# Attention and two feed-forward blocks on one core: how the folded matrix W is multiplied, and where weight blocks lie in SBUF

## The chip, the core and the metric

One core of a Trainium2 chip. The metric is device time of one execution in microseconds; the kernel before takes 933.91 us in the median of three runs. TensorE (PE) multiplies, VectorE (DVE), ScalarE (ACT) and GpSimd (POOL) work on tiles in SBUF, SyncE (SP) issues all the loads and stores.

## The reference, cut to what matters

```python
def _attn_ref(q, k, v):                 # B, H, S, D = 4, 8, 576, 64, all float32
    scores = scale * np.matmul(q, k.transpose(0, 1, 3, 2))
    mask = (rel >= 0) & (rel < 128)
    scores = np.where(mask, scores + bias, -1e9)      # bias: slope per head times distance
    attn = softmax(scores)
    return np.matmul(attn, v)

def _moe_ref(x, w1, w2, w3, w_out):     # x: 2304 x 512, d_ff 1024
    h = ((x @ w1) * (x @ w2)) @ w3
    return h @ w_out

def _moe2_ref(x, w_in, w_out):          # d_ff 2048
    h = x @ w_in
    return (h * np.clip(h + 3.0, 0.0, 6.0) / 6.0) @ w_out
```

The output is `_moe2_ref(_moe_ref(attention))`. In the text w_in and w_out of the last block are v_in and v_out.

## The kernel before

**Numbers.** Products are taken in float32 precision by splitting an operand into a high part (fp32r) and a low part, the remainder: `mm3` (L46) multiplies high by high, high by low and low by high, three matmuls for one. `split` (L68) makes the parts: a cast on ScalarE, a subtraction on another engine. Weights come from the host as 64-bit floats; `unpack` (L51) makes float32 of them in place, one step on ScalarE (L60) and two on VectorE (L61, L62). A block of 128 x 1024 weights thus costs five operations: three to unpack, two to split.

**Attention.** 16 head pairs (n = 0 to 15, four per batch), each in six slots (`attn_slot`): scores s_n_j for five blocks of 128 queries, softmax (biased scores pr, their minimum mn, sums sm, reciprocals rc), POOL's scaling by the reciprocal (L228), transposes (pt, th), the product with v (X_n_h for the two heads), and the split into xh and xl. The first four pairs are `whole`: their products are float32 matmuls on unsplit operands, such as s at L189 and X at L273; the other pairs use split operands. For whole pairs q is loaded to partitions 0 to 63, and k to both halves (L131 to 134); the other half of q is zeroed.

**W.** w3 and w_out are folded once: W = w3 @ w_out, 1024 x 512. `wo_unit` (L357) unpacks and splits four blocks of w_out to woh and wol, `w3_unit` (L361) eight blocks of w3 to w3h and w3l, `w_half` (L381) multiplies: eight row blocks wps0 to wps7, each eight times `mm3` at 512 columns. The result is split to Wh and Wl. `w12_unit` (L369) unpacks and splits the eight blocks of w1|w2.

**Order.** The list `queue` (L412) says in which order the 20 raw blocks are loaded: four of w_out, five of w3, three of w1|w2, three of w3; the other five blocks of w1|w2 follow in a loop at L449. They pass through two raw buffers (`rawp`, bufs=2): a load waits until the block two places earlier has been split. `work` spreads unpacking and W over 26 slots of attention (L438). The framework's scheduler then orders all instructions of each engine by priorities of its own; every engine, and SP's queue, works strictly in that order.

**Stages.** For each batch b and each half of its tokens, `ab_unit` multiplies x with a block of w1|w2 (two accumulators of 24 matmuls in all, in the two banks of `ps_mm`; asb on ScalarE and VectorE, then the split g), and `y_unit` multiplies with W. Attention of the next batch is interleaved. At the last batch the first three blocks of v_in|v_out and the first tokens of y are loaded and split ahead (L540 to 548), through one buffer (`dec`). The second block of layers then runs `h_unit` (h, rl, g2) and `o_unit` two behind it, for five blocks of 512 tokens; during the first of them the other 13 blocks of v_in|v_out are loaded, through the two buffers of `dec2`, and split, the low parts by POOL and VectorE in turn (L604 to 609).

## Time and profile before

| what | us |
|---|---|
| median of 3 runs | 933.91 (933.59 to 934.82) |
| the profiled execution | 938.28 |
| its span, first to last instruction | 936.5 |
| TensorE busy in the span | 892.5 (95%) |
| VectorE, ScalarE, POOL busy | 453.9, 416.2, 169.2 |
| mean granted clock of TensorE, share of full | 0.974 |

The profile is of one execution, and its times are those of that execution; the runs shown were timed without it. A matmul's end is modelled, so the spacing of starts tells what one costs; "idle before" is what an engine stood still ahead of an instruction, and the releaser is what it waited for last. PEclk is the granted clock of TensorE; 1.00 is the upper of its two levels (2.4 GHz), 0.50 the lower (1.2 GHz).

### The profile page before, as it was taken

To read this page: it belongs to the slowest core of one execution; us is meant where nothing else is said; L and a number is where in the kernel's file an instruction comes from. 1 tells how busy PE (TensorE), PEld (TensorE's weight loads), DVE (VectorE), ACT (ScalarE), POOL (GpSimd) and SP (SyncE) were. 2 spreads that over 40 slices of the span, in tenths; PEclk is the share of its full clock that TensorE was granted. 3 is DMA by queue.
4 is the path that set the end of the run, shared out by engine and by line. 5 is a ranking of instruction groups with operands and counts; after the bars stand their busy time and mean duration, and the time that the engine had idled before them with its cause. 6 is when DMAs were issued, how large, how long until landed. Compare 5 with 4: busy or idle time off the path is not lost.

```text
span 936.5 us, 13589 instructions
## 1 busy us (share of the span) xinstructions
PE 892.5 (95%) x5280; PEld 802.7 (86%) x5280; DVE 453.9 (48%) x940; ACT 416.2 (44%) x868; POOL 169.2 (18%) x230
## 2 busy tenths in 40 slices
PE   4798888999999999999999989999999999999998
PEld 3686667999999999999999978888888888888897
DVE  5768787647474656643422187842223222222232
ACT  5746666646464556543432266642223222222232
POOL 3311433312332333321020222230002001000000
PEclk8898878999999999999999989999999999999999
DMA  9674753212323233000430265410002000100010
GB/s 242 217 243 146 232 154 108 54 47 54 90 64 90 64 83 71 20 21 13 149 103 13 100 205 192 158 67 23 1 1 69 0 1 1 45 1 0 1 45 24
DMA packets 23473, 75.20 MB, mean 80 GB/s; under 512 B 2928, under 2 KB 8560, under 8 KB 18800
## 3 DMA queue, kind: packets, MB, share of 16 engines
...
q14 instruction: 24, 0.20, 0.1%
...
## 4 chain that ended last, share of the span: by engine, by line
PE 80%; DVE 1%; DMA 1%; ACT 1%; issue 0%; POOL 0%; DVEq 0%; ACTq 0%
PE o L47 7%; PE o L49 7%; PE o L48 7%; PE h L47 7%; PE h L49 7%; PE h L48 7%; PE ab L47 7%; PE ab L48 7%; PE ab L49 7%; PE y L47 3%; PE y L49 3%; PE y L48 3%; PE X L273 3%; PE pt L246 2%; PE s L191 1%; PE s L192 1%
## 5 line engine op out<-in xcount | busy, mean ns | idle before, releaser
L47 PE MATMUL ab<-xh,w12h 128*128 128x288 f32 x512 | 156.5, 306 | 1.7 <-ACT xh L68 0.9
L48 PE MATMUL ab<-xl,w12h 128*128 128x288 f32 x512 | 153.0, 299 | 0.0
L49 PE MATMUL ab<-xh,w12l 128*128 128x288 f32 x512 | 152.6, 298 | 0.0
L577 DVE SCALAR_TENSOR_TENSOR rl<-rl,h 128x512 f32<-128x512 f32 (+1 forms) x80 | 50.5, 633 | 178.6 <-ACT rl L576 178.6
L576 ACT ACTIVATE rl<-h,three 128x512 f32<-128x512 f32 (+1 forms) x80 | 51.5, 645 | 185.7 <-PE h L49 183.9
L47 PE MATMUL h<-yh,v2h 128*128 128x512 f32 (+1 forms) x320 | 118.7, 371 | 4.0 <-ACT v2h L68 4.0
L49 PE MATMUL h<-yh,v2l 128*128 128x512 f32 (+1 forms) x320 | 118.2, 369 | 0.0
L48 PE MATMUL h<-yl,v2h 128*128 128x512 f32 (+1 forms) x320 | 118.2, 369 | 0.0
L47 PE MATMUL o<-v2h,g2h 128*128 128x512 f32 x288 | 113.8, 395 | 0.0
L48 PE MATMUL o<-v2l,g2h 128*128 128x512 f32 x288 | 113.2, 393 | 0.0
L49 PE MATMUL o<-v2h,g2l 128*128 128x512 f32 x288 | 109.6, 394 | 0.0
L47 PEld LDWEIGHTS ab<-xh,w12h 128*128 128x128 f32 x512 | 97.5, 191 | 3.1 <-DVE asb L471 1.1
L48 PEld LDWEIGHTS ab<-xl,w12h 128*128 128x128 f32 x512 | 97.9, 191 | 0.0
L49 PEld LDWEIGHTS ab<-xh,w12l 128*128 128x128 f32 x512 | 97.7, 191 | 0.0
L228 POOL TENSOR_SCALAR pr<-pr,rc 128x256 f32<-128x256 f32 (+1 forms) x128 | 68.5, 554 | 156.2 <-DVE rc L221 132.9
L69 DVE TENSOR_TENSOR g2l<-rl,g2h 128x512 fp32r<-128x512 f32 (+1 forms) x80 | 57.9, 723 | 42.9 <-ACT g2h L68 42.7
L47 PE MATMUL y<-g,Wh 128*128 128x288 f32 x256 | 75.4, 298 | 0.0
L48 PE MATMUL y<-g,Wh 128*128 128x288 f32 x256 | 75.1, 295 | 0.0
L49 PE MATMUL y<-g,Wl 128*128 128x288 f32 x256 | 74.9, 295 | 0.0
L47 PEld LDWEIGHTS h<-yh,v2h 128*128 128x128 f32 x320 | 60.2, 188 | 15.2 <-ACT v2h L68 4.4
L48 PEld LDWEIGHTS h<-yl,v2h 128*128 128x128 f32 x320 | 60.3, 188 | 11.2
L519 POOL TENSOR_TENSOR yl<-yraw,yh 128x1024 fp32r<-128x1024 f32 (+1 forms) x10 | 23.3, 2348 | 256.3 <-ACT yh L518 256.3
...
## 6 DMA issues: line engine op xcount, KB each, us to landing
raww<-in_w_dram SPq DMA_DIRECT2D x16, 1024.0 KB, 5.3
rawv<-in_w2x_dram SPq DMA_DIRECT2D x16, 1024.0 KB, 4.7
...
rawwo<-in_wo_dram SPq DMA_DIRECT2D x4, 1024.0 KB, 8.9
yraw<-yT SPq DMA_DIRECT2D x4, 1024.0 KB, 5.2
```

Source lines behind the costliest of these rows:

```text
L47: nc.tensor.matmul(ps, lh, rh, start=first, stop=False)
L48: nc.tensor.matmul(ps, lh, rl, start=False, stop=False)
L49: nc.tensor.matmul(ps, ll, rh, start=False, stop=last)
L69: lo_eng.tensor_tensor(out=lo, in0=src, in1=f32(hi), op=ALU.subtract)
L191: nc.tensor.matmul(o, sp1["qs"][:, qc], sp1["kh"][:, kc], start=True, stop=False)
L192: nc.tensor.matmul(o, sp1["qs"][:, qc], sp1["kl"][:, kc], start=False, stop=True)
L228: nc.gpsimd.tensor_scalar(out=o, in0=o, scalar1=rc[:, 2 * j + h : 2 * j + h + 1], scalar2=1.0, op0=ALU.mult, op1=ALU.mult)
L246: nc.tensor.transpose(ps[:, o : o + P], prob[n, j][:, h, c : c + P], ident)
L273: nc.tensor.matmul(X[:, c0 : c0 + nq], l, r, start=bank not in seen, stop=last[bank] == idx, skip_group_check=True)
L519: nc.gpsimd.tensor_tensor(out=yl[:, c, 0:n], in0=t[:, c, 0:n], in1=f32(yh[:, c, 0:n]), op=ALU.subtract)
L576: nc.scalar.activation(rl[:, 0:n], ps[:, 0:n], AF.Relu, bias=three[:, 0:1], scale=1.0)
L577: nc.vector.scalar_tensor_tensor(out=rl[:, 0:n], in0=rl[:, 0:n], scalar=6.0, in1=ps[:, 0:n], op0=ALU.min, op1=ALU.mult)
```

## The change

1. **W.** w3 and w_out are only unpacked (`unpack` gets an output tile), and `w_half` multiplies them as whole float32 operands: 64 matmuls of 512 columns in place of 192. woh, wol, w3h, w3l and their splits are gone.
2. **Places.** A pool `blk` has 16 places of 4 KB per partition, hi0 to hi7 and lo0 to lo7, which live to the end of the program. w_out lies in hi4 to hi7 and w3 in lo4 to lo7 (four blocks at a time) until W is made; then w1|w2 blocks 4 to 7 take these. Blocks 3 to 10 of v_in|v_out take the places of w1|w2 blocks 0 to 7 when those are done with.
3. **Raw buffers.** Three in the first stage (`rawx` adds one). Four blocks of w1|w2 come ahead of the last three of w3, and the work is spread over 20 slots in place of 26 (`WEND`).
4. **v_in|v_out.** Blocks 0 to 10 and the first tokens of y are made during the last batch, after the units listed in `AT`, through two buffers; the rest during the first h units. All low parts are made by VectorE.
5. **k of whole pairs** is loaded to one half of the partitions; the other half is zeroed once, by POOL.

```diff
-    def unpack(raw):
+    def unpack(raw, out=None):
...
+        out = w0 if out is None else out.bitcast(I32)
         nc.vector.scalar_tensor_tensor(
-            out=w0, in0=w1, scalar=3, in1=w0, op0=ALU.logical_shift_left, op1=ALU.bitwise_or
+            out=out, in0=w1, scalar=3, in1=w0, op0=ALU.logical_shift_left, op1=ALU.bitwise_or
         )
...
+    blk = ctx.enter_context(tc.tile_pool(name="blk", bufs=1))
...
+    rawx = raw_ctx2.enter_context(tc.tile_pool(name="rawx", bufs=1, side="right"))
...
-            for a in range(1 if whole(n) and nm == "q" else 2):
+            for a in range(1 if whole(n) else 2):
...
     def wo_unit(i):
-        c = slice(2 * i, 2 * i + 2)
-        split(flat(woh[:, c, :]), flat(wol[:, c, :]), unpack(rawt.pop(("wo", i))), nc.vector)
+        t = blk.tile([P, 2, DM], F32, tag=f"hi{KH + i}", name=f"wov{i}")
+        unpack(rawt.pop(("wo", i)), flat(t))
+        wov[2 * i], wov[2 * i + 1] = t[:, 0, :], t[:, 1, :]
 
     def w3_unit(i):
-        hi = t2.tile([P, KF, P], F32R, tag="w3h", name=f"w3h{i}")
-        lo = t2.tile([P, KF, P], F32R, tag="w3l", name=f"w3l{i}")
-        split(flat(hi), flat(lo), unpack(rawt.pop(("w3", i))), nc.vector)
-        w3s[i] = (hi, lo)
+        t = blk.tile([P, KF, P], F32, tag=f"lo{KH + i % KH}", name=f"w3v{i}")
+        unpack(rawt.pop(("w3", i)), flat(t))
+        w3v[i] = t
...
-        for m in range(half * n, (half + 1) * n):
-            mm3(ps[:, 0:DM], hi[:, m, :], lo[:, m, :], woh[:, m, :], wol[:, m, :], m == 0, m == KF - 1)
+        for m in range(half * KH, (half + 1) * KH):
+            nc.tensor.matmul(ps[:, 0:DM], w3v[i][:, m, :], wov[m], start=m == 0, stop=m == KF - 1)
...
+    for q, kk in zip(qw, kw):
         nc.vector.memset(q[D:P, :], 0.0)
+        nc.gpsimd.memset(kk[D:P, :], 0.0)
...
+    queue = [("wo", i) for i in range(KH)] + [("w3", i) for i in range(KF)]
+    queue[-3:-3] = [("w12", f) for f in range(KH)]
...
+            load((k, i), {"wo": wo, "w3": w3, "w12": w12}[k][i], rawp, rawp, rawx)
...
-        upto = (s + 1) * len(work) // nslot
+        upto = (s + 1) * len(work) // (nslot - WEND)
...
+        old = NPRE <= f < NPRE + KF
+        hi, lo = (
+            (blk if old else pool).tile(
+                [P, 2 * KD, P], F32R, name=f"v2{t[0]}{f}", **({"tag": f"{t}{f - NPRE}"} if old else {})
+            ) for t in ("hi", "lo")
+        )
...
+            AT = [3, 6, 9, 11, 13, 15, 16, 18, 19, 20, 21, 22]
             pre = ctx.enter_context(tc.tile_pool(name="pre", bufs=1, side="right"))
-            dec = ctx.enter_context(tc.tile_pool(name="dec", bufs=1, side="right"))
+            dec = ctx.enter_context(tc.tile_pool(name="dec", bufs=2, side="right"))
...
+            if b == B - 1:
+                if iu in AT:
+                    p2_make(AT.index(iu), pre)
...
-            if f + NPRE < KG:
-                v2_split(f + NPRE, vpool, nc.vector if f % 2 else nc.gpsimd)
+            p2_make(f + len(AT), vpool)
```

How the change moves instructions shows in the order of each engine's queue.

**TensorE behind X_0_1**, the second head of pair 0. wps is the accumulator of a row block of W, wov and w3v the unpacked blocks, pt the transposes. Before:

```order
L273 MATMUL X_0_1_306<-th_0_1_1_253,vwrawv_97 128x64
L246 MATMUL pt_1_0_0_414<-ident_60,pr_1_2_361 128x128
L246 MATMUL pt_1_0_1_421<-ident_60,pr_1_2_361 128x128
L246 MATMUL pt_1_0_1_421<-ident_60,pr_1_3_369 128x128 x2
L246 MATMUL pt_1_1_0_438<-ident_60,pr_1_0_328 128x128
L246 MATMUL pt_1_1_0_438<-ident_60,pr_1_1_336 128x128 x2
L246 MATMUL pt_1_1_0_438<-ident_60,pr_1_2_361 128x128
L273 MATMUL X_1_0_481<-th_1_0_0_415,vwvs_98 128x256 x2
```

Now:

```order
L277 MATMUL X_0_1_290<-th_0_1_1_257,vwrawv_100 128x64
L389 MATMUL wps0_244<-wov0_164,w3v0_238 128x512 x2
L389 MATMUL wps0_244<-wov1_192,w3v0_238 128x512 x2
L389 MATMUL wps0_244<-wov2_198,w3v0_238 128x512 x2
L389 MATMUL wps0_244<-wov3_217,w3v0_238 128x512 x2
L250 MATMUL pt_1_0_0_391<-ident_60,pr_1_2_348 128x128
L250 MATMUL pt_1_0_1_398<-ident_60,pr_1_2_348 128x128
L389 MATMUL wps1_285<-wov0_164,w3v1_270 128x512 x2
L389 MATMUL wps1_285<-wov1_192,w3v1_270 128x512 x2
L389 MATMUL wps1_285<-wov2_198,w3v1_270 128x512 x2
L389 MATMUL wps1_285<-wov3_217,w3v1_270 128x512 x2
L250 MATMUL pt_1_0_1_398<-ident_60,pr_1_3_356 128x128 x2
```

W stood behind the transposes and products of pair 1 and the scores of pair 2; now three whole row blocks of it stand among the transposes of pair 1.

**VectorE at the scores of pair 2.** L203 before, and L207 now, is the biased score pr with its minimum mn; raww3_i and raww12_f are raw blocks, the subtraction into Wl is the end of a row block of W. Before:

```order
L61 TENSOR_SCALAR raww3_0_221<-raww3_0_221 128x1024
L62 SCALAR_TENSOR_TENSOR raww3_0_221<-raww3_0_221 128x1024
L258 COPY th_1_1_0_439<-pt_1_1_0_438 128x512
L220 TENSOR_SCALAR rc_2_520<-sm_2_519 128x4
L61 TENSOR_SCALAR raww3_1_243<-raww3_1_243 128x1024
L221 RECIPROCAL rc_2_520<-rc_2_520 128x4
L69 TENSOR_TENSOR w3l0_262<-raww3_0_221,w3h0_261 128x1024
L203 ISA pr_2_2_558,mn_2_518<-s_2_2_555,rel8_99 128x256
L203 ISA mn_2_518 128x1
L203 ISA pr_2_2_558,mn_2_518<-s_2_2_555,rel8_99 128x256
```

Now:

```order
L70 TENSOR_TENSOR Wl_95<-wps3_406,Wh_94 128x512
L61 TENSOR_SCALAR raww3_6_542<-raww3_6_542 128x1024
L63 SCALAR_TENSOR_TENSOR w3v6_622<-raww3_6_542 128x1024
L61 TENSOR_SCALAR raww3_7_564<-raww3_7_564 128x1024
L63 SCALAR_TENSOR_TENSOR w3v7_681<-raww3_7_564 128x1024
L61 TENSOR_SCALAR raww12_4_721<-raww12_4_721 128x1024
L207 ISA pr_2_2_513,mn_2_477<-s_2_2_510,rel8_102 128x256
L207 ISA mn_2_477 128x1
L207 ISA pr_2_2_513,mn_2_477<-s_2_2_510,rel8_102 128x256
L207 ISA mn_2_477 128x1
L63 SCALAR_TENSOR_TENSOR raww12_4_721<-raww12_4_721 128x1024
```

pr_2_2 stood behind the first block of w3 and the first step on the second; now it stands behind all eight of them, four of w1|w2 and the first step on a fifth (raww12_4).

**VectorE at the start of the second block of layers.** rawv2_f are raw blocks of v_in|v_out, g_3_1_7 the last product of ab, rl_0_0 the first result of h. Before:

```order
L471 TENSOR_TENSOR asb_3_1_7_5717<-ab1_3_1_7_5719,asb_3_1_7_5717 128x288
L69 TENSOR_TENSOR g_3_1_7_5732<-asb_3_1_7_5717,g_3_1_7_5732 128x288
L61 TENSOR_SCALAR rawv2_3_5866<-rawv2_3_5866 128x1024
L62 SCALAR_TENSOR_TENSOR rawv2_3_5866<-rawv2_3_5866 128x1024
L577 SCALAR_TENSOR_TENSOR rl_0_0_5890<-rl_0_0_5890,h_0_0_5877 128x512
L577 SCALAR_TENSOR_TENSOR rl_0_1_5919<-rl_0_1_5919,h_0_1_5906 128x512
L61 TENSOR_SCALAR rawv2_4_5868<-rawv2_4_5868 128x1024
L69 TENSOR_TENSOR g2l_0_0_5892<-rl_0_0_5890,g2h_0_0_5891 128x512
```

Now:

```order
L70 TENSOR_TENSOR g_3_1_7_5605<-asb_3_1_7_5590,g_3_1_7_5605 128x288
L63 SCALAR_TENSOR_TENSOR rawv2_9_5616<-rawv2_9_5616 128x1024
L70 TENSOR_TENSOR v2l9_5684<-rawv2_9_5616,v2h9_5683 128x1024
L61 TENSOR_SCALAR rawv2_10_5653<-rawv2_10_5653 128x1024
L63 SCALAR_TENSOR_TENSOR rawv2_10_5653<-rawv2_10_5653 128x1024
L70 TENSOR_TENSOR v2l10_5721<-rawv2_10_5653,v2h10_5720 128x1024
L61 TENSOR_SCALAR rawv2_11_5690<-rawv2_11_5690 128x1024
L63 SCALAR_TENSOR_TENSOR rawv2_11_5690<-rawv2_11_5690 128x1024
L70 TENSOR_TENSOR v2l11_5771<-rawv2_11_5690,v2h11_5770 128x1024
L61 TENSOR_SCALAR rawv2_12_5727<-rawv2_12_5727 128x1024
L63 SCALAR_TENSOR_TENSOR rawv2_12_5727<-rawv2_12_5727 128x1024
L599 SCALAR_TENSOR_TENSOR rl_0_0_5792<-rl_0_0_5792,h_0_0_5779 128x512
L599 SCALAR_TENSOR_TENSOR rl_0_1_5821<-rl_0_1_5821,h_0_1_5808 128x512
```

Before, one block (the fourth, rawv2_3) stood between the last g and rl_0_0; now rawv2_9 to rawv2_12 stand there. The blocks ahead of those stand among the last ab products, rawv2_5 ahead of asb_3_1_2 and so on.

## Rows read from the trace of the kernel before

**Rows 1.** By stretch: busy us (instructions) per engine, clock, DMA share, GB/s.

```profile
0.00:160.00 160.00, 124.23 (x597) 104.03 (x598) 117.87 (x254) 99.82 (x206) 48.67 (x78) 0.88 0.64 194
160.00:446.00 286.00, 286.00 (x2241) 285.55 (x2241) 158.71 (x445) 153.11 (x410) 78.02 (x136) 1.00 0.22 57
```

**Rows 2.** Timeline of TensorE: start, us, operation, [idle before <-releaser].

```profile
541.48 0.79 PE L47 MATMUL h<-yh,v2h 128*128 128x512 f32 x1 [3.96 <-ACT v2h L68]
```

**Rows 3.** Busy time by stretch, around 541 us.

```profile
532.00:541.00 9.00, 5.53 (x25) 4.23 (x23) 3.49 (x4) 5.26 (x7) 4.82 (x2) 0.97 0.83 287
541.00:548.00 7.00, 6.52 (x17) 5.13 (x18) 6.97 (x7) 4.99 (x7) 2.85 (x1) 0.56 0.63 226
```

**Rows 4.** Busy time by stretch, inside the first 160 us.

```profile
0.00:45.00 45.00, 26.82 (x118) 21.79 (x119) 28.91 (x81) 28.65 (x70) 14.53 (x33) 0.89 0.82 239
45.00:124.00 79.00, 70.60 (x329) 57.98 (x328) 56.93 (x108) 47.47 (x90) 21.77 (x28) 0.91 0.57 184
124.00:160.00 36.00, 26.81 (x154) 24.26 (x153) 32.03 (x66) 23.70 (x48) 12.37 (x17) 0.78 0.55 161
```

**Rows 5.** Waits of TensorE, 0 to 160 us: us in total, times, longest.

```profile
PE pt L246 <- POOL pr L228: 9.3, 7, 3.1
PE s L189 <- DMA kwrawk<-in_kT_dram: 8.0, 1, 8.0
```

**Rows 6.** Timeline of VectorE, 130 to 151 us.

```profile
132.90 0.82 DVE L69 TENSOR_TENSOR xl<-xf,xh 128x288 fp32r<-128x288 f32 x2
150.12 1.22 DVE L69 TENSOR_TENSOR w12l<-raww,w12h 128x1024 fp32r<-128x1024 f32 x1
```

**Rows 7.** Timeline of TensorE, 143 to 160 us.

```profile
143.94 0.29 PE L47 MATMUL ab<-xh,w12h 128*128 128x288 f32 x1
146.62 0.29 PE L49 MATMUL ab<-xh,w12l 128*128 128x288 f32 x1
159.38 0.59 PE L47 MATMUL ab<-xh,w12h 128*128 128x288 f32 x1
```

**Rows 8.** Tile wps: ns min/median/max, first to last start; then the timeline.

```profile
L47 PE MATMUL wps<-woh,w3h x64: 387/389/792, 45.5 to 122.2; 128*128 128x512 f32 x64
...
50.13 0.39 PE L48 MATMUL wps<-wol,w3h 128*128 128x512 f32 x1
52.40 0.39 PE L49 MATMUL wps<-woh,w3l 128*128 128x512 f32 x1
```

**Rows 9.** Timeline of TensorE, 25 to 28 us.

```profile
25.63 1.89 PE L189 MATMUL s<-kwkh,qwqs 128*128 128x256 f32 x8
27.36 0.49 PE L246 MATMUL pt<-ident,pr 128*128 128x128 f32 x3
27.68 0.27 PE L250 MATMUL pt<-ident,prt 128*128 128x128 f32 x1
```

**Rows 10.** Groups by line, 0 to 190 us: count, busy us, mean ns, idle.

```profile
L62 DVE SCALAR_TENSOR_TENSOR raww<-raww 128x1024 int32<-128x1024 int32 x16 | 20.9, 1305 | 3.6 <-ACT raww L60 3.5
L60 ACT ACTIVATE raww<-raww 128x1024 f32<-128x1024 f32 x16 | 18.8, 1174 | 17.9 <-DMA raww<-in_w_dram 17.9
L69 DVE TENSOR_TENSOR w12l<-raww,w12h 128x1024 fp32r<-128x1024 f32 x8 | 9.6, 1218 | 2.7 <-ACT w12h L68 2.7
L68 ACT CAST w12h<-raww 128x1024 fp32r<-128x1024 f32 x8 | 9.1, 1152 | 3.6 <-DVE raww L62 3.5
L228 POOL TENSOR_SCALAR pr<-pr,rc 128x256 f32<-128x256 f32 x42 | 23.5, 575 | 33.2 <-DVE rc L221 33.2
```

**Rows 11.** Timeline of TensorE, X_0_1 at 33 us.

```profile
32.73 2.07 PE L273 MATMUL X<-th,vwrawv 128*128 128x64 f32 x12
```

**Rows 12.** Timelines of ScalarE and POOL, 1 to 6 us.

```profile
2.97 2.56 ACT L400 ACTIVATE rel<-relm 128x256 bf16<-128x256 f32 x8 [0.95 <-POOL relm L394]
...
1.39 0.20 POOL L403 MEMSET vwrawv<- 64x128 f32 x1
```

**Rows 13.** DMA issues of the page: count, size, median us to landing.

```profile
rawv<-in_w2x_dram SPq DMA_DIRECT2D x16, 1024.0 KB, 4.7
```

More of the change, by code (lines that the diff above doesn't have):

```diff
@@ L82, in tile_attention_moe_moe2 @@
     xpool = p1.enter_context(tc.tile_pool(name="xpool", bufs=1))
-    w12a = p1.enter_context(tc.tile_pool(name="w12a", bufs=1))
     apool_ctx = ExitStack()
@@ L405, in tile_attention_moe_moe2 @@
     nc.gpsimd.memset(three, 3.0)
-    load(("wo", 0), wo[0], rawp)
-    load_hp(0, "v")
-    load(("wo", 1), wo[1], rawp)
-    load_hp(1, "qk")
-    NA = 3
-    g0 = 0
-    queue = [("wo", i) for i in range(KF // 2)]
-    for i in range(KF):
-        queue += [("w3", i)]
-    queue[-3:-3] = [("w12", f) for f in range(NA)]
-    nxt = 2
+    queue = [("wo", i) for i in range(KH)] + [("w3", i) for i in range(KF)]
+    queue[-3:-3] = [("w12", f) for f in range(KH)]
+    nxt = 0
     def more():
@@ L421, in more @@
             k, i = queue[nxt]
-            load((k, i), {"wo": wo, "w3": w3, "w12": w12}[k][i], rawp)
+            load((k, i), {"wo": wo, "w3": w3, "w12": w12}[k][i], rawp, rawp, rawx)
             nxt += 1
+    more()
+    load_hp(0, "v")
+    more()
+    load_hp(1, "qk")
+    more()
     work = []
@@ L428, in tile_attention_moe_moe2 @@
     nslot = SLOTS * NP + 2
+    WEND = 6
     def do_work(w):
@@ L433, in do_work @@
             return
-        {"wo": wo_unit, "w3": w3_unit, "w12": lambda f: w12_unit(f, w12a)}[w[0]](w[1])
+        {"wo": wo_unit, "w3": w3_unit, "w12": w12_unit}[w[0]](w[1])
         more()
     wi = 0
+    rest = False
     for s in range(nslot):
-        attn_slot(g0 + s)
-        upto = (s + 1) * len(work) // nslot
-        while wi < upto:
+        attn_slot(s)
+        upto = (s + 1) * len(work) // (nslot - WEND)
+        if wi < len(work) and upto >= len(work):
+            rest = True
+        while wi < min(upto, len(work)):
             do_work(work[wi])
             wi += 1
-    tmp_ctx.close()
-    w12b = p1.enter_context(tc.tile_pool(name="w12b", bufs=1))
+        if rest:
+            rest = False
+            raw_ctx2.close()
+            for f in range(KH, KF):
+                load(("w12", f), w12[f], rawp)
+                w12_unit(f)
     sp = p1.enter_context(tc.tile_pool(name="sp", bufs=2))
-    for f in range(NA, KF):
-        load(("w12", f), w12[f], rawp)
-        w12_unit(f, w12b)
     raw_ctx.close()
@@ L494, in v2_split @@
     def v2_split(f, pool, lo_eng):
-        hi = pool.tile([P, 2 * KD, P], F32R, name=f"v2h{f}")
-        lo = pool.tile([P, 2 * KD, P], F32R, name=f"v2l{f}")
+        old = NPRE <= f < NPRE + KF
[4 more added lines that the diff above has]
+        )
         split(flat(hi), flat(lo), unpack(rawt.pop(("v2", f))), lo_eng)
@@ L503, in tile_attention_moe_moe2, with p2_load, p2_make @@
     yraw = {}
+    p2 = [("v", f) for f in range(KG)]
+    p2.insert(NPRE, ("y", 0))
+    def p2_load(i):
+        if i < len(p2):
+            (v2_load if p2[i][0] == "v" else y_load)(p2[i][1], dec)
+    def p2_make(i, pool):
+        if i < len(p2):
+            if p2[i][0] == "v":
+                v2_split(p2[i][1], pool, nc.vector)
+            else:
+                y_split(0, pool)
+            p2_load(i + 2)
     def y_load(j, tmp):
@@ L522, in tile_attention_moe_moe2 @@
     SKEW = 3
-    PST = 4
     units = []
@@ L558, in tile_attention_moe_moe2 @@
     r2 = ctx.enter_context(tc.tile_pool(name="r2", bufs=2))
-    dec2 = ctx.enter_context(tc.tile_pool(name="dec2", bufs=2))
     g2p = ctx.enter_context(tc.tile_pool(name="g2p", bufs=3))
@@ L604, in tile_attention_moe_moe2 @@
         if j == 0:
-            for i in range(NPRE, NPRE + 2) if f == 0 else [f + NPRE + 1]:
-                if NPRE <= i < KG:
-                    v2_load(i, dec2)
-            if f + NPRE < KG:
-                v2_split(f + NPRE, vpool, nc.vector if f % 2 else nc.gpsimd)
+            p2_make(f + len(AT), vpool)
         h_unit(j, f)
```

44 lines of the change are left out of this document (18 added, 26 removed).

## The prediction

> **What bounds the kernel now.** I read the busy times by stretch first. Between 160 and 446 us TensorE is busy 286.00 of 286 us at the full clock, while the first 160 us hold 124.23 us of its work, at a mean clock of 0.88 [rows 1]. So the later stages can only be shortened by taking matmuls away, and the change takes none away there. Time can come from the first 160 us, and from one hole at the start of the second feed-forward: TensorE stands still for 3.96 us before an h product that waits for the cast of v2h, block 3 of v_in|v_out [rows 2], and the next stretch runs at clock 0.56 [rows 3].
>
> In the first stretch the work is spread unevenly: 0 to 45 us has 18 us without TensorE, 45 to 124 us has 8, 124 to 160 us has 9 and a clock of 0.78 [rows 4]. The waits name the softmax chain (9.3 us for POOL's normalised rows) and the first keys (8.0 us) [rows 5]. Neither is the product W; W fills time in which attention can't keep TensorE busy. What ends the stretch is that VectorE and ScalarE are still unpacking weights: the last w12l is written at 150 us, 17 us after the last half of the batch's x (xl, 133 us) [rows 6], and TensorE runs unbroken from 159.38 us [rows 7].
>
> **W: three products become one.** Before, 192 matmuls of 512 columns; ten of them take 2.27 us [rows 8], so 0.227 each, 43.6 us. A whole float32 matmul stands in the trace as two records (the program has four of these where the trace has eight); eight records of 256 columns take 1.73 us [rows 9], 0.216 each, so one matmul costs 0.432 per 256 columns. No row has 512 columns; I take twice that, 0.864, and 64 of them cost 55.3 us. The bounds are the same columns at half and at one and a half of it for a weight load that hides or doesn't: minus 16 to plus 39 us against before; the nearest rows (same type, half the width) give plus 11.7, which I take. The Trainium skill ("FP8 and Floating Point Precision", TensorE Precision Notes) counts four passes for true float32; an estimate by it is 64 x 4 x 0.227 = 58.1, plus 14.5 instead of plus 11.7. No run here has that operation yet.
>
> **What leaves VectorE and ScalarE.** Twelve blocks (4 of w_out, 8 of w3) lose their cast and subtraction: with 1.15 and 1.22 us [rows 10] that is 13.8 us of ScalarE and 14.6 of VectorE in the first stage. That is not the gain; it only shortens what TensorE waits for.
>
> **The first stage, walked in the new order.** TensorE now starts W right behind X_0_1, which ended at 34.8 us before [rows 11], and no longer at 45.5 [rows 8]. From there to the last matmul of W stand 55.3 us of W, 28 other float32 matmuls of 5248 columns in all (X of head pairs 1 and 2, scores of 2 and 3: 8.9 us at 0.432 per 256) and 29 transposes (0.11 each by their spacing in [rows 9], 3.2 us): W ends at 34.8 + 67.4 = 102.2 us; before at 123. Then VectorE has 53 instructions from pr_3_2 to the last xl of the batch; at the stage's mean of 117.87 / 254 = 0.464 us [rows 1] they take 24.6 us. Add 1.3 for the last Wh and Wl (a cast and a subtraction of 512 columns, half of those in [rows 10]) and 2.9 for POOL's normalising in between (five of 0.575 [rows 10]): 131.0 us. From there all eight w1|w2 blocks lie split and TensorE has ab units without end.
>
> Before, the same state is reached later. At 159.38 us TensorE had done, beyond what the new order has done then, 54 matmuls of ab (20 take 2.68 us [rows 7]; 7.2 us), 24 of X_4 and 20 scores (44 of at most 256 columns, 0.12 in proportion; 5.0 us) and 18 transposes (2.0): 14.2 us. So a start at 145.2 would be worth the same, and 131.0 wins **14.2 us**. Off this go 2 us for the clock: between 102 and 131 TensorE has little to do, and after the hole of 3.96 us seven microseconds ran at 0.56 [rows 3], worth 3.1; the bounds are 0 and 3.1. Another 3 go for the loads. In VectorE's new queue pr_2_2 stands behind the first step on raww12_4, the 17th megabyte, and TensorE needs it for s_2_4 at about 79 us. With q, k, v that is 21.1 MB: at 239 GB/s (0 to 45 us) 88 us, at 287 GB/s (532 to 541 us) 74 us [rows 3, 4]. So 0 to 9, and I take 3, as three loads now overlap. One microsecond comes back early: four subtractions of w_out (5 us of VectorE) stood before X_0_1; bounds 0 and 5. The first stage gives **10.2**.
>
> **At nothing:** the two memsets of the k tiles on POOL stand ahead of the mask that rel8 is made from. rel8 ends at 5.53 us, the first keys are there at 8.0 [rows 5, 12]. A memset of 64x128 took 0.20 us [rows 12]; at nine times the columns two of them cost at most 3.6, the cover is 2.5, so 0 to 1.1. The half of k no longer loaded twice is worth 0 to 0.6 us at the start. I take 0 for the pair.
>
> **The hole at 537 us.** v2_3 to v2_10 go to the places of finished w1|w2 blocks and are made during the last batch, so the h units no longer wait for a load. That returns 3.96 and, of the 7.0 us at clock 0.56, 3.1: 7.1. What is late next: two buffers now serve these blocks, and one turn is a load of 4.7 us [rows 13] and 4.9 us of unpacking (1.17, 1.30, 1.15, 1.22 in a row [rows 10]), so a block comes every 4.8 us while an ab unit lasts 24 x 0.134 = 3.2 us. VectorE's queue puts rawv2_5 before asb_3_1_2 and so on, and TensorE has only two banks for ab. Following five blocks through I find 2 us of waits; bounds 0 and 8 (five times 1.6). And rl_0_0 stands behind rawv2_12: h_0_4 needs the bank of h_0_0 5.4 us into the stage, the twelfth block is there some 2.4 us later. Bounds 0 and 4. Net **2.7**.
>
> **Sum:** 10.2 + 2.7 = 12.9 us. The profiled execution took 938.28 us (span 936.5), which is 4.4 above the median of the runs, 933.91; I take the same gain off the median: **921.0 us**. About 0.2% (1.9 us) is what a measurement can tell from no change.
>
> **Rivals.**
> 1. TensorE starves after W. W now ends before head pair 3 has begun its softmax, so the filler is gone where before wps5 to wps7 lay. For it: s_3_2 stands behind Wl of the last product in VectorE's queue. If the chain of 29 us takes 38, the first stage gives 1 to 3 us and the time is 927 to 932; typically 930.
> 2. More than forecast: loads keep up, the clock stays, no waits in the ab units. 14.2 + 5 + 7.1, less some 2, is 24: 910. At TensorE's own work alone from 102 us the ab units could start at 117 us, 14 earlier still; nothing speaks for that, since the softmax is a chain.
> 3. Slower: the loads set the pace. At the 184 GB/s of 45 to 124 us [rows 4] the 21.1 MB come at 115 us instead of 79, TensorE stands behind s_2_4 with 21 matmuls of W still to do (18 us), and the chain of 27 follows: 160 against 145.2, that is 15 lost, less 2.7: 946. It decides from about 90 us on for raww12_4. Against it: between 45 and 124 us the DMA engines were only 57% busy, so they waited for buffers, and there are three now. The Trainium skill ("DMA: Bandwidth & Descriptors", Where 436 GB/s comes from) gives about 358 GB/s per core for loads from HBM; an estimate by it is 59 us for the 21.1 MB, and this rival could not occur. The trace stays below that rate over each whole stretch shown here.
> 4. Two stages cancel: the ab units lose their 8 us, the loads their 9, and the time is within 2 us of before. Also here: the float32 product of 512 columns costs half as much again, 28 us more, of which the slack between 102 and 131 hides only part.
>
> **Chances.** Forecast (914 to 927): 0.48. Rival 1 (927 to 932): 0.20. Rival 2 (905 to 914): 0.18. Rival 4: 0.06. Rival 3: 0.08. Faster by over 0.2%: 0.86; within: 0.06; slower: 0.08. The range 907 to 931 leaves out the two last rivals (0.14), and some 0.06 of the ends of rivals 1 and 2.
>
> **What will show it.** Right: W's matmuls at 0.43 us a record between about 35 and 105 us; the last w12l near 115 us and not 150; TensorE without a pause from about 133 us; no hole at the first h units after y. Wrong: a TensorE wait of over 5 us for pr_2_2 or the loads near 80 us; W ending later than 115 us; waits of ab for asb in the last batch adding up to over 4 us; the span shrinking in the stages between 160 and 446 us, for which I have no reason.

## The result, and the profile after

| | before | changed |
|---|---|---|
| time, median (runs) | 934.2 us (933.59 to 934.82, 4) | 924.79 us (920.97 to 925.85, 4) |
| ratio, 95% interval | | 0.9886 (0.9856 to 0.9915) |
| profiled execution, its span | 938.28, 936.5 us | 920.97, 919.1 us |

The changed kernel is about 1.1% faster: 9.4 us off the median, where 12.9 were forecast (921.0 us, range 907 to 931). The two profiled executions are 17.3 us apart, because that of before lies 4 us above its median and that of after 4 us below its own. What differs between executions is the first thing to explain, so parts of the trace are compared below by their lengths and not by their place in the span alone.

The busy times by stretch of the changed kernel (busy us and instructions of TensorE, its weight loads, VectorE, ScalarE and POOL; granted clock, DMA share, GB/s) answer to [rows 1, 4]:

```profile
0.00:45.00 45.00, 34.07 (x129) 22.58 (x130) 30.42 (x75) 26.88 (x62) 18.65 (x35) 0.96 0.95 322
45.00:124.00 79.00, 74.20 (x282) 46.86 (x280) 54.80 (x119) 45.70 (x93) 19.99 (x28) 0.94 0.47 162
124.00:160.00 36.00, 32.82 (x238) 31.85 (x239) 24.66 (x59) 19.75 (x54) 13.70 (x20) 0.95 0.34 83
0.00:160.00 160.00, 141.10 (x647) 101.29 (x648) 109.88 (x252) 92.33 (x207) 52.33 (x83) 0.95 0.58 189
160.00:446.00 286.00, 284.39 (x2232) 283.93 (x2231) 165.61 (x446) 158.13 (x412) 77.45 (x133) 1.00 0.26 71
```

TensorE has 141.1 us of work in the first 160 in place of 124.2, at a clock of 0.95 in place of 0.88. From 160 to 446 us it is still full. The loads of the first 45 us run at 322 GB/s in place of 239. VectorE's work in the first 160 us fell by only 8 us, since work of later stages has moved in.

TensorE's waits in those 160 us (total, times, longest) answer to [rows 5]; POOL's 9.3 us have shrunk to 1.5:

```profile
PE s L193 <- DMA kwrawk<-in_kT_dram: 5.9, 1, 5.9
PE s L193 <- DMA kwkh<-in_kT_dram: 3.6, 1, 3.6
PE ab L47 <- ACT xh L69: 3.1, 2, 1.8
PE pt L250 <- POOL pr L232: 1.5, 4, 0.5
```

Of TensorE's timeline, one product of W, answering to [rows 8], and then of VectorE's timeline the last w12l and the last x halves of the batch, answering to [rows 6]:

```profile
37.72 7.03 PE L389 MATMUL wps<-wov,w3v 128*128 128x512 f32 x16
44.59 0.38 PE L250 MATMUL pt<-ident,pr 128*128 128x128 f32 x2
```

```profile
109.12 1.84 DVE L70 TENSOR_TENSOR w12l<-raww,w12h 128x1024 fp32r<-128x1024 f32 x1
128.75 0.82 DVE L70 TENSOR_TENSOR xl<-xf,xh 128x288 fp32r<-128x288 f32 x2
```

Sixteen records take 44.59 - 37.72 = 6.87 us, 0.429 each: a whole float32 matmul of 512 columns costs 0.858 us, 64 of them 54.9. W runs from 30.5 to 98.2 us. The last w12l is written at 109 us and no longer at 150, the last xl at 129.6, and from there TensorE works without a pause.

Around the place where the hole was, by stretch as in [rows 3], there is no idle time left and the clock is full; TensorE's only waits between 400 and 600 us stand below it:

```profile
532.00:541.00 9.00, 9.00 (x41) 7.40 (x40) 8.40 (x11) 6.82 (x9) 0.00 (x0) 1.00 0.55 210
541.00:548.00 7.00, 7.00 (x32) 5.71 (x32) 5.21 (x7) 4.95 (x6) 0.46 (x1) 1.00 0.51 166
```

```profile
PE h L47 <- DVE rl L599: 2.2, 1, 2.2
PE ab L47 <- DVE asb L478: 1.6, 1, 1.6
PE ab L47 <- ACT asb L475: 0.2, 1, 0.2
```

**Two parts that can be measured apart.** From the last y matmul to the last matmul of the program there are no loads of the first stage, and in two traces of the changed kernel the length differs by 0.6 us. The last y and the last two matmuls, before and then after:

```profile
531.78 0.29 PE L49 MATMUL y<-g,Wl 128*128 128x288 f32 x1
931.86 0.61 PE L49 MATMUL o<-v2h,g2l 128*128 128x512 f32 x2
```

```profile
520.86 0.29 PE L49 MATMUL y<-g,Wl 128*128 128x288 f32 x1
913.86 0.61 PE L49 MATMUL o<-v2h,g2l 128*128 128x512 f32 x2
```

Before, this part goes from 531.8 to 932.1 us (starts of the two matmuls): 400.3 us. After, from 520.9 to 914.1: 393.2 us. Some h matmuls already stand ahead of the last y, 12 before and 24 after, and they are work of this part done early. So I add 0.227 us for each: 403.0 and 398.7 us, **4.3 us won in the second part**. What is left of the medians is the first part: 936.0 (17 executions, experiment 1) less 403.0 is 533.0 us; 924.2 (the middle of ten executions of the changed kernel) less 398.4 (the mean of its two traces) is 525.8 us: **7.2 us won**. This is good to some 2 us, since the interval of the ratio in experiment 1 alone is 9 to 14 us for the whole.

### The profile page after: what moved, and what is told of

Same layout as the page of the kernel before. It is cut to its first block, busy times and chain, and to the rows that moved or that the text cites. A ratio compares the mean times of both kernels' runs of the same rounds, so it can differ in the third digit from the quotient of the medians.

```text
span 919.1 us, 13413 instructions
## 1 busy us (share of the span) xinstructions
PE 891.5 (97%) x5216; PEld 782.5 (85%) x5216; DVE 439.6 (48%) x935; ACT 402.2 (44%) x856; POOL 152.0 (17%) x225
## 4 chain that ended last, share of the span: by engine, by line
PE 89%; DMA 4%; DVE 3%; ACT 1%; issue 1%; POOL 1%; SPq 0%; DVEq 0%; ACTq 0%; POOLq 0%
PE o L47 7%; PE o L49 7%; PE o L48 7%; PE h L47 7%; PE h L48 7%; PE h L49 7%; PE ab L47 7%; PE ab L48 7%; PE ab L49 7%; PE wps L389 6%; PE X L277 4%; PE y L47 3%; PE y L48 3%; PE y L49 3%; DMA rawv<-in_w2x_dram 3%; PE pt L250 3%
## 5 line engine op out<-in xcount | busy, mean ns | idle before, releaser
L70 DVE TENSOR_TENSOR g2l<-rl,g2h 128x512 fp32r<-128x512 f32 (+1 forms) x80 | 54.7, 684 | 47.3 <-ACT g2h L69 47.1
## 6 DMA issues: line engine op xcount, KB each, us to landing
rawwo<-in_wo_dram SPq DMA_DIRECT2D x4, 1024.0 KB, 10.2
```

Of the source, the lines that this page charges most:

```text
L70: lo_eng.tensor_tensor(out=lo, in0=src, in1=f32(hi), op=ALU.subtract)
```

## The experiments

**1. The changed kernel again.** No edit. 

> The changed kernel once more, unaltered, for a second trace and more times. Theory A (its executions differ by the granted clock in the stretch between the end of W and the unbroken ab units): again 920 to 926 us, and where an execution is longer its mean clock is lower (0.986 where 0.990 is the fastest); a second trace differs from the first by over 1 us between 95 and 145 us or around 525 us only. Theory B (they differ by the loads): W starts or ends at another time than 30.5 and 98.2 us, by more than 2 us.

Six executions: 923.7 us (922.14 to 929.1), ratio 0.9877 (0.9852 to 0.9902) over 17 executions of the kernel before (936.0). Its profiled execution happened to be the longest, 929.1. Its first 45 us by stretch, and one step of VectorE there, first as it was in the earlier trace (18.26 us) and then in this one:

```profile
0.00:45.00 45.00, 29.09 (x109) 21.23 (x110) 25.32 (x69) 22.95 (x57) 16.52 (x35) 0.85 0.89 271
```

```profile
18.26 0.86 DVE L61 TENSOR_SCALAR rawwo<-rawwo 128x1024 int32<-128x1024 int32 x1 [1.79 <-DMA rawwo<-in_wo_dram]
24.06 0.70 DVE L61 TENSOR_SCALAR rawwo<-rawwo 128x1024 int32<-128x1024 int32 x1 [4.92 <-DMA rawwo<-in_wo_dram]
```

The loads ran at 271 GB/s in place of 322: the first block of w_out, asked for at 1.97 us in both traces, landed at 10.5 us in place of 8.9. VectorE stood 4.9 us before the third, with the biased scores of pair 1 and a copy of pair 0's transposes behind it in its queue. W started at 37.8 us and not at 30.5; from there on the two traces run alike (67.1 us from W's first to its last start in both, and 398.1 and 398.7 us for the second part). Theory B holds; why the loads were slower, no run shows. The mean clock doesn't order the executions: one of 926.12 us had the highest, 0.994.

**2. Whole products alone, in the kernel before.**

```diff
...
-            mm3(ps[:, 0:DM], hi[:, m, :], lo[:, m, :], woh[:, m, :], wol[:, m, :], m == 0, m == KF - 1)
+            nc.tensor.matmul(ps[:, 0:DM], t[:, m, :], wov[:, m, :], start=m == 0, stop=m == KF - 1)
```

> The kernel before with one edit: w3 and w_out are only unpacked and W is made from whole float32 products; places, two raw buffers, the order of the w1|w2 blocks (three in phase W, five behind it) and the hole at the first h units stay. Theory A (what VectorE and ScalarE no longer do for twelve blocks is what makes the first stage shorter, though TensorE gets 11 us more): 924 to 929 us, last w12l between 118 and 135 us, unbroken ab units from 138 to 150 us. Rival B (third raw buffer and shared places do it, the whole products only cost): 932 to 942 us, the last w12l at 145 us or later. Rival C (the gain of the change is all in the hole): 934 us, no change.

936.57 us, ratio 1.0012 (0.9997 to 1.0028): no change. W's matmuls, the w12l, the last x half of the batch, and the wait at the first h units:

```profile
L384 PE MATMUL wps<-wov,w3v x128: 592/592/1061, 35.7 to 109.2; 128*128 128x512 f32 x128
```

```profile
L70 DVE TENSOR_TENSOR w12l<-raww,w12h x8: 1211/1223/1304, 63.0 to 137.7; 128x1024 fp32r<-128x1024 f32 x8
```

```profile
144.24 1.12 DVE L70 TENSOR_TENSOR xl<-xf,xh 128x288 fp32r<-128x288 f32 x1
```

```profile
PE h L47 <- ACT v2h L69: 3.9, 1, 3.9
```

W starts 10 us earlier than before and ends 13 earlier, the last w12l comes 12 us earlier, and yet nothing is won. The last xl, which W now stands in front of, is done at 145.4 us, 12 later than before. TensorE's lost time in the first 160 us (counted as in experiment 8) is some 12 us less, but it has 54.9 - 43.6 = 11.3 us more to do, and that eats it. Theory A, which was the prediction's, falls. Rival B's time came out, but not its w12l.

**3. The changed kernel with two raw buffers.**

```diff
...
-            load((k, i), {"wo": wo, "w3": w3, "w12": w12}[k][i], rawp, rawp, rawx)
+            load((k, i), {"wo": wo, "w3": w3, "w12": w12}[k][i], rawp)
```

> The changed kernel with two raw buffers in place of three. Theory A (loads overlap better with three, but VectorE's work sets most of the pace): 925 to 929 us, that is 1 to 4 more than the change; W starts 2 to 6 us later than 30.5 us and ends later by less than that. Rival B (the third buffer is the whole gain of the first stage): 931 to 936 us, W starts near 40 us or later. Rival C (it does nothing): within 1.5 us of the change.

929.21 us, ratio 0.9929 (0.9904 to 0.9954): 5.5 us are lost against the changed kernel measured beside it (experiment 1). Its first 45 us show 262 GB/s:

```profile
0.00:45.00 45.00, 32.42 (x125) 23.14 (x126) 26.62 (x78) 25.47 (x65) 16.36 (x35) 0.92 0.85 262
```

The loss is nearly half of what the change wins. It lies between A (1 to 4 more) and B. The rate is no evidence for the buffer: the changed kernel's own two traces show 322 and 271, and W's start, 34.5 us here, lies between their 30.5 and 37.8. The loss is read from the times.

**4. The same buffer in the kernel of experiment 2.** Whole products free the low parts' room there too, so a third raw buffer fits.

```diff
...
+    rawx = raw_ctx2.enter_context(tc.tile_pool(name="rawx", bufs=1, side="right"))
-            load((k, i), {"wo": wo, "w3": w3, "w12": w12}[k][i], rawp)
+            load((k, i), {"wo": wo, "w3": w3, "w12": w12}[k][i], rawx if nxt % 3 == 2 else rawp)
```

> The kernel before with whole float32 products for W and a third raw buffer during phase W (the whole products free the room for it); the places of w1|w2, of v_in|v_out and the hole at the first h units stay. Theory A (the third raw buffer is worth 5 us wherever W is whole): 929 to 933 us, W starts 2 to 7 us earlier than the 35.7 us of the same kernel with two; the hole of 3.9 us stays. Rival B (in the old places the last five blocks of w1|w2, which come after phase W, end the stage whatever the loads do): 934 to 937 us, last w12l within 3 us of 137.7.

931.47 us, ratio 0.9952 (0.9932 to 0.9973): 5.1 us off experiment 2 (4.2 if each is taken against the kernel before that was measured beside it), with the hole still there and the last w12l hardly moved (135.9 in place of 137.7), but the last xl 9 us earlier:

```profile
L70 DVE TENSOR_TENSOR w12l<-raww,w12h x8: 1194/1219/1236, 56.2 to 135.9; 128x1024 fp32r<-128x1024 f32 x8
```

```profile
135.09 0.83 DVE L70 TENSOR_TENSOR xl<-xf,xh 128x288 fp32r<-128x288 f32 x2
```

Theory A's time holds: the buffer is worth some 5 us in either arrangement, and the last w12l, where Rival B had expected it, isn't what ends the stage. But A's sign did not come: W starts at 37.3 us, 1.6 later than in experiment 2 and not 2 to 7 earlier. The gain lies behind W's start. From its first to its last start W takes 67.4 us in place of 73.6; a wait of 3.0 us of W for w3v is gone, and the waits for POOL's rows are 2.0 us in place of 9.2.

**5. Split products in the shared places, two raw buffers.** Three products with split operands in the changed kernel; they leave room for two raw buffers and for three early blocks of w1|w2.

```diff
...
-        t = blk.tile([P, 2, DM], F32, tag=f"hi{KH + i}", name=f"wov{i}")
-        unpack(rawt.pop(("wo", i)), flat(t))
...
+        hi = blk.tile([P, 2, DM], F32R, tag=f"hi{KH + i}", name=f"woh{i}")
+        lo = blk.tile([P, 2, DM], F32R, tag=f"lo{KH + i}", name=f"wol{i}")
+        split(flat(hi), flat(lo), unpack(rawt.pop(("wo", i))), nc.vector)
...
```

> The changed kernel with two raw buffers and with W from three split products again (w_out's halves in the shared places, w3's in two places of which one is that of w12_3, so three blocks of w1|w2 are made early and five behind W). To be compared with the changed kernel with two raw buffers, 929.2 us. Theory A (whole products take more off VectorE and ScalarE than they cost TensorE): 933 to 940 us, W starts 5 us or more later than 34.5 and the last w12l comes later than 120 us. Rival B (11 us more of TensorE pay for all that the whole products save, as in the kernel before with whole products alone, which took as long as before): 927 to 931 us.

927.28 us, ratio 0.9911 (0.9878 to 0.9943), against 0.9929 (0.9904 to 0.9954) with whole products: no difference that the intervals allow to see. Here too one arrangement starts W late and is done late with w1|w2, as Theory A had it, and ends level:

```profile
L47 PE MATMUL wps<-woh,w3h x64: 387/389/628, 45.8 to 113.9; 128*128 128x512 f32 x64
```

```profile
L70 DVE TENSOR_TENSOR w12l<-raww,w12h x8: 1214/1224/1227, 73.5 to 139.3; 128x1024 fp32r<-128x1024 f32 x8
```

Theory A falls, rival B holds. With two raw buffers whole products win nothing in the old places or in the new. Split products with three were not run: the places of w3's two parts lie where the third buffer lay.

**6. Half of W.** In `w_half` every second m is left out.

```diff
...
-        for m in range(half * KH, (half + 1) * KH):
+        for m in range(half * KH, (half + 1) * KH, 2):
...
```

> The changed kernel without every second product of W (32 whole float32 matmuls in place of 64), so W holds half of its sum; all loads, unpacking and everything else stay. TensorE has 27.5 us less to do before 98 us. Theory A (TensorE sets the pace from W's start to its end): W ends 12 to 25 us earlier and the time falls by 8 us or more, to 916 or less. Rival B (loads and the softmax chain of pairs 2 and 3 set it, and W only fills): W ends at most 8 us earlier and the time falls by 0 to 6 us, 918 to 924.

907.22 us, ratio 0.9681 (0.9655 to 0.9708). Of the 27.5 us taken off TensorE 16.5 come out in the time, so Theory A holds in the time: between W's start and its end TensorE is the bound, and each microsecond taken off it there is worth 0.6. W's end came 11.3 us earlier (86.9 us), just short of A's 12, since W started at 34.2 us here. The changed kernel's own trace shows the same, from W's start to its end and from there to the last xl:

```profile
30.50:98.20 67.70, 67.67 (x213) 35.99 (x214) 46.00 (x82) 36.34 (x62) 16.89 (x20) 1.00 0.66 236
98.20:129.60 31.40, 23.43 (x119) 19.39 (x118) 24.30 (x59) 19.08 (x47) 11.91 (x18) 0.83 0.28 81
```

The last xl of the batch came at 119.4 us, 10 earlier:

```profile
118.56 0.85 DVE L70 TENSOR_TENSOR xl<-xf,xh 128x288 fp32r<-128x288 f32 x2
```

So W stands in front of the softmax chain of pairs 2 and 3 in TensorE's queue. After W there is too little to do until that chain is through. Experiment 10 uses this.

**7. The table of places cut.** `AT` ends after its fourth entry, so in program order v2_3 and the later blocks are made only from the first h unit on.

```diff
-            AT = [3, 6, 9, 11, 13, 15, 16, 18, 19, 20, 21, 22]
+            AT = [3, 6, 9, 11]
```

> The changed kernel with the table of places cut to its first four entries: v2_0 to v2_2 and y_0 are made in the last batch, v2_3 and all others from the first h unit on, as before the change (two of them are loaded ahead). Theory A (making them early takes away the hole): a wait of the h product for v2h or v2l of 2 to 5 us comes back after the last y unit, the waits of ab for asb (1.8 us) go, 1 to 4 us more than the change in all. Rival B (the hole was only the load, and two blocks loaded ahead cover it): no h product waits over 1 us, and the time is 0 to 3 us below the change, since the ab units lose their waits. The first 400 us are as in the change by either.

923.54 us, ratio 0.987 (0.9847 to 0.9893): as the change. TensorE's waits are the same three (asb 1.8 and 0.2, rl 1.7 us), and the second part takes 398.2 us. The blocks are still made from 485 us on, during the last ab units: the scheduler brings them forward, since their places come free. So neither theory's case arose, and the table doesn't decide.

**8. Places of their own for v2_3 and later.** The pool of shared places closes with the first feed-forward, as before, and `AT` is cut as in 7.

```diff
...
-        old = NPRE <= f < NPRE + KF
+        old = False
...
```

> The changed kernel, but v2_3 to v2_15 get places of their own again, which come free only when the tiles of the first feed-forward are given back; v2_0 to v2_2 and y_0 are made ahead as before. Theory A (the shared places are what takes the hole away, since the scheduler can then bring the blocks forward; the table of places is not): an h product waits 3 to 5 us for v2h again, TensorE's lost time between 446 and 640 us grows from 6 to 9 to 11 us, total 926 to 929 us. Rival B (two blocks loaded ahead are enough): no such wait, 922 to 925 us. Up to 446 us the same as the change by either.

922.12 us, ratio 0.9848 (0.9818 to 0.9877). I had expected the hole back. It isn't: between 500 and 532 us TensorE is busy throughout, and ScalarE casts two blocks in a row:

```profile
500.00:532.00 32.00, 32.00 (x206) 29.90 (x205) 11.82 (x18) 12.78 (x21) 0.00 (x0) 1.00 0.23 85
```

```profile
520.61 2.16 ACT L69 CAST v2h<-rawv 128x1024 fp32r<-128x1024 f32 x2
```

TensorE's lost time between 446 and 640 us (the time that goes by, less the matmuls started in it at their spacing at the full clock) is 2.4 us, where the changed kernel has 5.8. The places come free with the last y unit at 519.9 us. v2_3 and v2_4 are by then loaded (landed at 452.0 and 457.5 us) and unpacked in the two raw buffers, and all that remains is their cast and subtraction. Before, the loads were issued only then (532.1 and 533.0 us, the last y at 531.8), since their buffers were opened together with these places. Rival B holds: the hole was the load alone. And the second part takes 396.3 us, against 398.7 with the shared places: nothing but the blocks in use is made ahead, VectorE is free when rl_0_0 comes, and the wait of 2.2 us is gone. The wait of ab for asb stays (1.7 us).

**9. Pair 4's splitting held back.** Between W's end and the last xl VectorE and ScalarE also split q and k of the next batch's first pair. Here that is pinned behind the x halves of pair 3, and the loads of pair 5's q and k follow it.

```diff
...
+            pin = tc.keep_in_program_order if n == NP else (lambda i: i)
-            nc.scalar.activation(qs[:, c], r[:, c], AF.Copy, scale=sc)
+            pin(nc.scalar.activation(qs[:, c], r[:, c], AF.Copy, scale=sc))
...
```

> The changed kernel; only the order of VectorE and ScalarE is another: the splitting of head pair 4's q and k (4 instructions on each engine, about 4 us, pair 4 belongs to the next batch) is held behind the x halves of pair 3. Theory A (from W's end to the first unbroken ab unit the time is a chain through VectorE and ScalarE, and this work stands in it twice): the last xl of the batch comes 3 to 8 us earlier than 31 us behind W's end, 916 to 921 us. Rival B (the splitting of w12_4 to w12_7 or POOL sets that stretch): last xl within 2 us, 922 to 925 us. Rival C (pair 4's scores come too late and TensorE waits for them later): the wait shows as s of pair 4 waiting for kl after the ab units began, 922 us or more.

925.87 us, ratio 0.988 (0.9847 to 0.9913): no gain. The chain did get shorter. W ended at 101.5 us and the last xl was done at 126.9, 25.5 us later in place of 31.4:

```profile
124.76 2.19 DVE L70 TENSOR_TENSOR xl<-xf,xh 128x288 fp32r<-128x288 f32 x2
```

But 28 matmuls of pair 4's scores stood between 106 and 130 us in the changed kernel and 2 here. They filled TensorE's waits there and now stand behind them. By stretch, first the changed kernel, then this one:

```profile
100.00:130.00 30.00, 22.03 (x109) 18.12 (x108) 23.15 (x58) 17.99 (x45) 10.27 (x17) 0.81 0.26 71
```

```profile
100.00:130.00 30.00, 20.75 (x103) 16.73 (x102) 18.66 (x36) 13.78 (x27) 8.54 (x15) 0.91 0.22 69
```

109 matmuls against 103: no more work is done by the same time (W ends 3 us later in this trace). From W's start to the last matmul the traces take 882.1 us here and 883.6 and 884.4 in the changed kernel, so a gain of 2 us may hide in the spread, not one of 6. Rival C comes nearest, though no wait shows it: shortening a chain wins nothing if the work that filled its waits leaves with it.

**10. The tail of W as filler.** On the kernel of experiment 8, the last two of W's eight products are held behind the last scores of pair 3.

```diff
...
+        pin = tc.keep_in_program_order if i in TAIL_W else (lambda i: i)
-            nc.tensor.matmul(ps[:, 0:DM], w3v[i][:, m, :], wov[m], start=m == 0, stop=m == KF - 1)
+            mm = nc.tensor.matmul(ps[:, 0:DM], w3v[i][:, m, :], wov[m], start=m == 0, stop=m == KF - 1)
+            if m == half * KH:
+                pin(mm)
...
+    TAIL_W = [6, 7]
+        if s == 20:
+            for i in TAIL_W:
+                w_half(i, 0)
+                w_half(i, 1)
...
```

> The kernel of the run own_places with the last two of W's eight products (13.8 us of TensorE) held behind the last scores of head pair 3, so that they fill the wait for pair 3's softmax. Theory A (after W's end TensorE waits for a chain that W stands in front of; without 27.5 us of W the x of pair 3 was ready 10 us earlier): W ends near 105 us, the last xl of pair 3 comes at 119 to 125 us instead of 130, TensorE's lost time at 140 us falls from 45 to 34 to 41 us, 912 to 919 us. Rival B (W's tail holds back w12_4 to w12_7, whose places it uses, and the ab units wait for them): last w12l after 122 us and an ab wait for it, 919 to 924 us. Rival C (VectorE is the chain, W's place does not matter): 920 to 924 us, last xl at 128 us or later.

**915.32 us (914.04 to 916.61, 5 executions), ratio 0.9786 (0.9767 to 0.9806): faster than both kernels.** W's matmuls and the last xl:

```profile
L390 PE MATMUL wps<-wov,w3v x128: 592/592/697, 33.2 to 105.6; 128*128 128x512 f32 x128
```

```profile
125.51 0.83 DVE L70 TENSOR_TENSOR xl<-xf,xh 128x288 fp32r<-128x288 f32 x2
```

W ends at 106.2 us, 6 later than in experiment 8, and yet the last xl is done 4.6 us earlier (126.3 in place of 130.9), and the time is 6.8 us less (5.5 if each is taken against the kernel before that was measured beside it). The spread of the first loads has no part in it: from W's start to the last matmul the two traces take 874.4 and 880.9 us. TensorE's lost time in the first 140 us is 5.5 us less. Theory A holds; the xl came 1 us later than its range. The last w12l comes at 119.5 us, before Rival B's 122, and no ab unit waits for it.

**11. Three products held back.** `TAIL_W = [5, 6, 7]`. 

> As tail67_own, with the last three products of W (20.6 us) held behind the last scores of pair 3. Theory A: xl of pair 3 as early as in tail67_own or 1 to 4 us earlier, but W ends 2 to 6 us later, and w12_4 to w12_7 with it: within 4 us of tail67_own on either side. Rival C of tail67_own: 920 to 926 us.

922.58 us, ratio 0.9868 (0.9834 to 0.9903), 7 us worse than with two; I had expected at most 4. The stretch from 66 to 100 us, in the kernel of experiment 10 and then in this one:

```profile
66.00:100.00 34.00, 33.76 (x129) 20.85 (x128) 21.89 (x56) 18.35 (x45) 8.79 (x17) 1.00 0.55 169
```

```profile
66.00:100.00 34.00, 29.79 (x107) 18.51 (x107) 20.97 (x55) 16.97 (x43) 8.71 (x17) 0.90 0.55 170
```

With 20.6 us of W held back TensorE runs dry ahead of pair 3's scores (4.2 us idle, clock 0.90, 22 matmuls fewer). The scores don't come earlier for it, W ends at 113.5 us and the last xl at 133.4. Three products are more than that wait takes.

**12. Keys of pair 1 first.** On the kernel of experiment 10, the loads of q and k of pair 1 are issued ahead of v and of the second block of w_out.

```diff
...
     more()
+    load_hp(1, "qk")
     load_hp(0, "v")
     more()
-    load_hp(1, "qk")
     more()
...
```

> The kernel of the run tail67_own (915.3 us) with one more edit in the order of the loads: q and k of head pair 1 are asked for ahead of v of pair 0 and of the second block of w_out. Theory A (the scores of pair 1 wait 3 to 5 us for their keys, and that delays the chain that W's start follows): the wait for the keys of pair 1 falls below 2 us, W starts 1 to 4 us before 33.2 us, 911 to 914.5 us. Rival B (the loads of the first 30 us run one behind the other, so what comes earlier makes w_out later, and VectorE stands before it): the wait moves to VectorE's unpacking of w_out, W starts at 33 us or later, 914.5 to 919 us.

916.67 us, ratio 0.9805 (0.978 to 0.9829): no gain. TensorE's longest waits in its first 180 us:

```profile
PE s L193 <- DMA kwrawk<-in_kT_dram: 6.5, 1, 6.5
PE pt L250 <- POOL pr L232: 4.1, 5, 2.1
PE s L193 <- DVE mn L207: 3.2, 3, 1.4
```

The wait for pair 1's keys (4.6 us in experiment 10) is gone, and most of these microseconds stand at POOL (4.1 in place of 1.0 us) and VectorE (3.2 in place of 1.1); W starts at 33.9 us in place of 33.2. Rival B holds in the time and in W's start; the wait moved to steps of the softmax, and W's own wait for unpacked weights is 0.5 us.

## Why the prediction was right, and where it was not

The direction, the range and the size hold: 12.9 us forecast, 9.4 measured at first and 12.3 in experiment 1. The reasons hold in part, and that the sum fits is partly luck, since its two halves miss in opposite ways: 10.2 and 2.7 us forecast, 7.2 and 4.3 measured. By the prediction's own steps:

- **The price of W: right.** 55.3 us forecast, 54.9 measured. The Trainium skill ("FP8 and Floating Point Precision", TensorE Precision Notes) counts four passes. The runs fit that number with 0.858 / 4 = 0.215 us for a pass, where the estimate took the spacing of single matmuls, 0.227.
- **The walk through the first stage: its places right.** W's end was forecast for 102.2 us (98.2; 105.5 in experiment 1), the last w12l for near 115 (111.0), the last xl for 131.0 (129.6), 28.8 us behind W's end (31.4). That X_0_1 ends at 34.8 us as before was the uncertain number: W started at 30.5 and at 37.8 us in two executions. (The 1.3 us for the last Wh and Wl is 1.2 by its own rows.)
- **The comparison with before: right in the traces.** It said that unbroken ab units from 145.2 us on would be worth the kernel before. The kernel of experiment 2 has its last xl at 145.4 us and takes as long as the kernel before. In the two profiled executions the first part is 13.1 us shorter (936.5 - 403.0 against 919.1 - 398.7), where the comparison with 129.6 gives 15.6, less the wait for asb of 1.6. In the medians it is 7.2. The gain was worked out on an execution of 938.28 us, 2.3 above the median of 17, and taken off the median all the same; an estimate from these numbers is that some 2 of the 3.0 us that are missing lie there.
- **What the first stage gives: the cause was wrong.** The prediction walked from an early W and a lighter VectorE to a gain of 14.2 us, and took the third raw buffer into account only as a reason for taking 3 us of late loads and not more. Experiment 2 has the early W and the lighter VectorE, and wins nothing; experiments 3 and 4 put 5.5 and 5.1 us on the buffer. By the first part of each (median less the second part of its trace): before 533, whole products 533.4, with the third buffer 528.1, changed kernel 525.8 us. So whole products 0, the buffer about 5, places and order about 2, each good to some 2 us. What whole products do is to free room: without the low parts the buffer fits. The step that failed is the walk's length where the buffer is left out: 67.4 us from W's start to its end and 28.8 from there to the last xl were put down to the lighter engines. With two buffers, in experiment 2, they are 74.2 and 35.5 us; with the third, in experiment 4, 68.0 and 30.6.
- **The deductions.** Of the 3 us for late loads nothing shows: s_2_4 ran at 74.91 us (forecast about 79) without a wait. The loads did vary, but ahead of W, in the first 30 us. As to the 2 us for the clock, TensorE ran at 0.81 of its clock between 100 and 130 us in the changed kernel; no run here prices that.
- **The hole: right in its sizes, wrong in its cause.** Returned 7.1 forecast; the second part is 6.7 us shorter in experiment 8, which has neither hole nor rl wait. Waits of ab for asb 2 forecast, 1.8 in the trace; rl_0_0 behind rawv2_12 forecast 2.4, in the trace 2.2. The asb waits lie in the first part, so the second should give 7.1 - 2.4 = 4.7, and gives 4.3. But it was put down to blocks made in the places of finished w1|w2, and experiment 8 shows that two raw buffers that are loaded ahead are enough. The shared places bring the wait for rl_0_0, not the gain. The wait for asb isn't theirs: it comes at 442 us, where VectorE unpacks one of the first three blocks, and experiment 8 has it too; the late ab units, for which it was forecast, wait for nothing.
- **At nothing.** In the times the memsets of k on POOL and the half of k loaded once can't be told apart; the trace has both. The memsets took 1.05 us each, 2.1 against at most 3.6, and rel8 ends at 7.8 us in place of 5.5. The halved load is worth more at the start than the 0 to 0.6 us that were forecast: in experiment 2, with k loaded twice, the second half lands 1.2 us behind the first (7.0 and 5.8 us). Together, the first scores start at 5.9 us in place of 8.0 (7.1 in experiment 2) and the first biased score at 7.3 in place of 9.3 (8.5).
- **The rivals.** Rival 1, that TensorE starves after W, holds as a mechanism and not as a time: experiment 10 wins 6.8 us by putting W's tail there. Rival 2, W's end soon followed by ab units, needed a shorter chain; experiment 9 shows why that alone would not have paid. Rival 3, loads that set the pace up to 90 us, did not occur. Of the 8 us that Rival 4 gave the ab units 1.8 showed.

Left open: what share of the 2.3 us between experiment 4 and the changed kernel belongs to the places, to the order of w1|w2 or to k's loads; the runs don't resolve it.

## What to carry to other kernels

Price a dearer instruction at what it frees elsewhere, the room in SBUF included. Here whole products cost TensorE what they saved the other engines, and their worth was the raw buffer that fitted afterwards. If an engine is the bound in one stretch and starves in the next, move work that nobody waits for from the first to the second, and look first at what holds places that others wait for. When a hole stands before a transformed block, ask whether the load or the place was late; loading ahead into a buffer is the smaller change.

## What the runs showed of the chip

In the two traces of the changed kernel the first 45 us decide by how much they differ: 322 against 271 GB/s and 7 us in W's start, with everything behind it alike to a microsecond (883.6 and 884.4 us from W's start to the last matmul). I had looked for that in the clock. Within those 45 us the rate isn't even. The loads' view of the changed kernel between 8 and 16 us gives the busy share of the DMA engines and GB/s in 40 slices of 0.2 us:

```profile
DMA  9998999889789799989999999999787989899999
GB/s 520 369 328 348 448 433 451 328 369 573 328 369 492 315 387 364 294 179 207 184 230 207 207 230 184 261 274 228 187 251 228 392 269 410 369 451 410 451 410 451
```

From 11.4 to 14.2 us the engines are as busy as before and after, at about 215 GB/s in place of about 400. That is 0.6 MB, the size of q and k of pair 1 (288 KB each, to partitions 0 to 63), which the queue of loads has there between blocks of w_out to 128: the loads land at 13.0 (w_out), 14.4 and 15.6 (q and k) and 18.2 us (w_out). The Trainium skill ("SBUF — State Buffer", Door 1: The DMA port swizzle) says that a load's rate hangs on how many of 16 ports its partitions reach, and that partitions 0 to 63 reach half. The slices agree with that; no run here changed the layout of q and k to show it. The rows of q and k are shorter too, 4.5 KB for a partition against 8, and no run separates the two. The other slices go up to well over 358 GB/s, the rate that the prediction set against Rival 3, so that rate is no ceiling here.
